# Scaling a broadcast matrix by fp32 row factors: eight small products or one, and which engine empties PSUM

## Chip, core and metric

The kernel runs on one core of one Trainium2 chip. The metric is the time of one execution on the device, in microseconds (us); the median of several executions is given. A core has TensorE (matrix products, results in PSUM), VectorE (DVE in the profile), ScalarE (ACT), GpSimd (POOL) and SyncE (SP); the last two mainly start DMA transfers in the part that matters here.

## The reference

Four layers act on x, which has 2048 rows of 1024 bf16 values. Layers A multiply a two-dimensional Fourier transform by a filter; layers B are a dense network with the Mish activation. Each works on the normalised rows.

```python
def _A_ref(x, w_r, w_i):
    X = rfft2(x.astype(float32))          # over rows and columns
    X = X * (w_r + 1j * w_i)
    return irfft2(X, s=(S, D)).astype(bfloat16)

def _B_ref(x, w1, b1, w2):
    h = x @ w1 + b1                        # 1024 -> 3584
    act = h * tanh(softplus(h))
    return act @ w2                        # 3584 -> 1024

x = x + _A_ref(layernorm(x), A_w_r, A_w_i)
x = x + _B_ref(layernorm(x), B_w1, B_b1, B_w2)
x = x + _A_ref(layernorm(x), A_w_r, A_w_i)
x = x + _B_ref(layernorm(x), B_w1, B_b1, B_w2)
```

## The kernel before

The Fourier transform is done as matrix products with constant tables. The first step, `s1`, takes 128 products of 128x128 matrices: for each n, `XR[:, n, :]` (a slice of x) with one constant matrix `M0`. In the first layer x comes straight from the input and is not yet normalised. Rather than normalise x, the kernel scales the matrix: `MN[:, n, :] = M0 * rc[:, n]`, where `rc` is fp32 and holds one factor for every partition and every n (1 over the standard deviation of a row). So 128 scaled copies of `M0` have to be made, in 16 blocks of eight.

`first_scales` computes the statistics of the rows and leaves the factors in `RT`:

```python
self.op(dve, lambda e: e.tensor_copy(rt.ap, self.RS[:, 2, :].unsqueeze(2).to_broadcast([P, 16, 8])), ...)   # L557
self.group([lambda e: e.transpose(self.PS[:, 7, 0:P], rt.ap..., self.IDF.ap)], ...)                          # L560
self.op(dve, lambda e: e.tensor_copy(rt.ap..., self.PS[:, 7, 0:P]), ...)                                     # L562
```

`scaled(j)` makes the eight matrices of block j, two thirds of them on VectorE and one third on ScalarE:

```python
def scaled(self, j):
    rt = self.RT
    rc = rt.ap.rearrange("p a b -> p (a b)")
    for q in range(8):
        n = 8 * j + q
        if q % 3 == 1:
            self.op(self.act, lambda e, n=n: e.activation(self.MN.ap[:, n, :], self.M0.ap, ACT.Copy, scale=rc[:, n:n + 1]), ...)        # L576
        else:
            self.op(self.dve, lambda e, n=n: e.tensor_scalar(self.MN.ap[:, n, :], self.M0.ap, rc[:, n:n + 1], None, op0=ALU.mult), ...) # L579
```

`s1` makes the matrices of four blocks ahead. For each block it runs eight products into a pair of PSUM banks (four pairs in rotation), moves the 1024 results of each partition to `Y` in SBUF as bf16, and makes the matrices of the block four further on. In the second layer A (`li` is 1) x is already normalised, and one matrix `M` serves for all.

```python
def s1(self, li):
    ...
    for j in range(4 if not li else 0):
        self.scaled(j)
    for j in range(16):
        ps, banks, _ = self.pair()
        for q in range(8):
            n = 8 * j + q
            m = M[:] if li else self.MN.ap[:, n, :]
            # matmul(ps[:, q * P:(q + 1) * P], XR.ap[:, n, :], m)                                   L594
        self.group(fns, reads=[self.r_xr[j // 4], self.r_m if li else self.r_mn[j]], writes=banks)
        ...
        if j % 2 or li and j == 8:
            # activation(dst, src, ACT.Copy): ScalarE empties the pair                               L600
        else:
            # tensor_copy(dst, src): VectorE empties the pair                                        L602
        if not li and j + 4 < 16:
            self.scaled(j + 4)
```

`[... cut ...]` After `s1` comes the transform along the other axis, `s2` (matmuls L675, evacuated by ScalarE at L710), which reads all of `Y`; the filter's rows, copied by VectorE (L899) and turned by TensorE (L888); the later steps (L720 to L798, among them the bf16 products with the filter on VectorE, L731 to L738); and a round trip through `u_scratch` in HBM. Its results go into x at L933, and the dense layer follows (L994 and L1012).

Of the kernel before, what the change touches and what calls it, by code (L numbers as in the profile page):

```python
# [6 lines left out]
ALU = mybir.AluOpType  # L7
P = 128
# [171 lines left out]
class KB:  # L180
# [389 lines left out]
    def scaled(self, j):  # L570
        rt = self.RT
        rc = rt.ap.rearrange("p a b -> p (a b)")
        for q in range(8):
            n = 8 * j + q
            if q % 3 == 1:
                self.op(self.act, lambda e, n=n: e.activation(self.MN.ap[:, n, :], self.M0.ap, ACT.Copy, scale=rc[:, n:n + 1]),  # L576
                        reads=[rt.res, self.M0.res], parts=[self.r_mn[j]])
            else:
                self.op(self.dve, lambda e, n=n: e.tensor_scalar(self.MN.ap[:, n, :], self.M0.ap, rc[:, n:n + 1], None, op0=ALU.mult),  # L579
                        reads=[rt.res, self.M0.res], parts=[self.r_mn[j]])  # L580

    def s1(self, li):
        self.Y = self.alloc("Y", self.o["Y"], [P, P])
        self.Y.res.begin()
        M, XR = self.M, self.XR
# [4 lines that stand above are left out]
            fns = []  # L590
# [3 lines that stand above are left out]
                fns.append(lambda e, q=q, n=n, ps=ps, m=m: e.matmul(ps[:, q * P:(q + 1) * P], XR.ap[:, n, :], m,  # L594
                                                                   start=True, stop=True))
            self.group(fns, reads=[self.r_xr[j // 4], self.r_m if li else self.r_mn[j]], writes=banks)
            src = ps.rearrange("p (q k) -> p k q", q=8)
            dst = self.Y.ap[:, :, 8 * j:8 * j + 8]
            if j % 2 or li and j == 8:
                self.op(self.act, lambda e, dst=dst, src=src: e.activation(dst, src, ACT.Copy), reads=banks, parts=[self.Y.res])  # L600
            else:
                self.op(self.dve, lambda e, dst=dst, src=src: e.tensor_copy(dst, src), reads=banks, parts=[self.Y.res])  # L602
            if not li and j + 4 < 16:
                self.scaled(j + 4)
        for r in ([self.MN.res, self.M0.res] + self.r_xr if not li else []):
            r.r(self.pe, self.pe.count)
            self.XR.res.r(self.pe, self.pe.count)
# [593 lines left out]
```

## Time and profile before

| | |
|---|---|
| time, median of 3 | 1047.37 us (1046.68 to 1048.07) |
| span of the profiled execution | 1044.8 us |
| TensorE busy | 951.7 us, 91% of the span |
| VectorE busy | 350.9 us, 34% |
| ScalarE busy | 336.4 us, 32% |
| mean granted TensorE clock | 0.971 of full speed |

The profile names each group of instructions by the line of the kernel, the engine, the operation, and output and input by buffer: most SBUF tiles lie in one large buffer and appear as ARENA, and PSUM as PS. Each row gives the count, the busy time, the mean duration of one, and how long the engine stood idle before them. Neighbouring instructions of one engine overlap a little, so their spacing is shorter than their duration. The chain is the path that ended last: at each step, what released the work, or what stood ahead of it on its engine. The granted clock is the share of full speed that TensorE was given. A view by windows gives the busy time of each engine in a stretch of the span.

### The profile page before, as it was taken

How to read it: one execution, taken by the hardware profiler on the slowest of the kernel's cores; microseconds unless marked ns; L12 is line 12 of the kernel's file. 1: busy time of each engine (PE TensorE's matmuls, PEld its weight loads, DVE VectorE, ACT ScalarE, POOL GpSimd, SP SyncE). 2: the span in 40 equal slices, each digit the busy share in tenths (PEclk: the TensorE clock that was granted, in tenths of full speed). 3: DMA queues.
4: the chain of work that ended last, by engine and by line, in shares of the span. 5: the costliest groups of instructions: out<-in, count | busy, mean ns of one | idle time of the engine just before them, and what ended most of it. 6: DMA issues, size and time to landing. Idle time of an engine off the chain costs nothing.

```text
span 1044.8 us, 14118 instructions
## 1 busy us (share of the span) xinstructions
PE 951.7 (91%) x5944; PEld 510.5 (49%) x6033; DVE 350.9 (34%) x776; ACT 336.4 (32%) x503; POOL 71.1 (7%) x114
## 2 busy tenths in 40 slices
PE   0799489999999999999979957999999999999998
PEld 0567465444444444444447736644444444444443
DVE  6888462431433100033337756426011100000111
ACT  6898163332000333400009834533300013440000
POOL 3242000000000000001621200000000000000000
PEclk9699789999999999999989988999999999999999
DMA  9779822464111121001941874145611112200000
GB/s 284 172 252 284 194 80 91 152 195 139 46 52 43 51 81 41 1 11 40 219 84 64 231 190 126 42 151 182 195 26 45 45 64 81 61 1 11 21 21 31
DMA packets 153055, 107.02 MB, mean 102 GB/s; under 512 B 74384, under 2 KB 132064, under 8 KB 152992
## 3 DMA queue, kind: packets, MB, share of 16 engines
q1 hardware_dynamic: 141472, 77.04, 26.0%
q0 software_dynamic: 9488, 27.68, 9.0%
q10 hardware_dynamic: 2032, 1.39, 0.5%
q8 instruction: 48, 0.79, 0.3%
q14 instruction: 15, 0.12, 0.0%
HBM read 80.85 MB, written 20.71 MB: 97 GB/s over the span
## 4 chain that ended last, share of the span: by engine, by line
PE 80%; DVE 9%; ACT 6%; DMA 3%; issue 1%; ACTq 0%; DVEq 0%
PE PS L994 37%; PE PS L1012 37%; DVE BN L460 2%; ACT ARENA L727 2%; PE PS L675 2%; DVE XS L933 1%; DVE ARENA L579 1%; DVE ARENA L796 1%; DMA ARENA<-u_scratch 1%; DMA u_scratch<-ARENA 1%; ACT ARENA L710 1%; DVE ARENA L969 1%; DVE ARENA L602 1%; PE PS L919 1%; ACT ARENA L798 1%
## 5 line engine op out<-in xcount | busy, mean ns | idle before, releaser
L994 PE MATMUL PS<-ARENA 128*128 128x512 bf16 (+1 forms) x1946 | 391.0, 360 | 10.3 <-DVE ARENA L969 7.2
L1012 PE MATMUL PS<-ARENA 128*128 128x512 bf16 x1756 | 385.5, 379 | 1.9
L998 ACT ACTIVATE ARENA<-PS,B 128x512 bf16<-128x512 f32 (+1 forms) x248 | 159.8, 646 | 438.8 <-PE PS L994 438.7
L994 PEld LDWEIGHTS PS<-ARENA 128*128 128x128 bf16 x1984 | 194.2, 99 | 202.2 <-DVE ARENA L969 8.7
L1012 PEld LDWEIGHTS PS<-ARENA 128*128 128x128 bf16 x1792 | 175.4, 98 | 211.4
L1017 DVE TENSOR_TENSOR XS<-PS,XS 128x512 bf16<-128x512 f32 x64 | 44.3, 692 | 537.9 <-PE PS L1012 537.9
L460 DVE BATCH_NORM_STATS2 BN<-XS 128x6 f32<-128x512 bf16 x104 | 67.2, 675 | 7.6 <-DMA XS<-in_A_x_dram 6.3
L933 DVE TENSOR_TENSOR XS<-PS,XS 128x512 bf16<-128x512 f32 (+1 forms) x40 | 29.1, 790 | 82.9 <-PE PS L919 82.9
L919 PE MATMUL PS<-MT,ARENA 128*128 128x32 bf16 (+1 forms) x768 | 24.3, 187 | 27.4 <-DMA ARENA<-u_scratch 24.7
L919 PEld LDWEIGHTS PS<-MT,ARENA 128*128 128x128 bf16 x768 | 22.9, 100 | 30.8 <-issue 25.0
L441 ACT ACTIVATE ARENA<-XS 128x1024 bf16<-128x1024 bf16 x24 | 25.3, 1055 | 37.3 <-DVE XS L933 32.4
L727 ACT ACTIVATE ARENA<-PS 128x1024 bf16<-128x1024 f32 x32 | 33.9, 1060 | 8.5 <-PE PS L723 8.5
L675 PE MATMUL PS<-FD,ARENA 128*128 128x256 bf16 (+1 forms) x256 | 33.8, 279 | 2.9 <-ACT ARENA L600 1.2
L756 ACT ACTIVATE ARENA<-PS 128x1024 bf16<-128x1024 f32 x32 | 33.9, 1061 | 3.7 <-PE PS L749 3.7
L432 ACT ACTIVATE RS<-MV,EPS 128x1 f32<-128x1 f32 (+1 forms) x7 | 2.0, 292 | 98.7 <-DVE MV L463 96.2
L749 PE MATMUL PS<-ARENA 128*128 128x256 bf16 x256 | 33.2, 273 | 0.1
L249 POOL DMA_DIRECT2D xn_scratch<-ARENA x12 | 6.5, 543 | 391.0 <-DVE ARENA L499 391.0
L731 DVE TENSOR_TENSOR ARENA<-ARENA 128x1024 bf16<-128x1024 bf16 x32 | 22.0, 687 | 22.0 <-ACT ARENA L727 22.0
L749 PEld LDWEIGHTS PS<-ARENA 128*128 128x128 bf16 x256 | 24.5, 98 | 10.0 <-DVE ARENA L738 1.2
L675 PEld LDWEIGHTS PS<-FD,ARENA 128*128 128x128 bf16 x256 | 24.6, 101 | 8.4 <-DVE ARENA L602 2.8
L770 PE MATMUL PS<-ARENA,BD 128*128 128x256 bf16 x192 | 25.9, 273 | 1.3 <-DVE ARENA L796 1.0
L499 DVE TENSOR_SCALAR ARENA<-XS,MV,RS 128x1024 bf16<-128x1024 bf16 x48 | 25.0, 543 | 1.0
(70 smaller groups left out, 502.8 us busy)
## 6 DMA issues: line engine op xcount, KB each, us to landing
ARENA<-in_B_w_dram SPq DMA_DIRECT2D x56, 512.0 KB, 4.0
ARENA<-in_B_w_dram SPq DMA_DIRECT2D x56, 256.0 KB, 4.5
u_scratch<-ARENA SPq DMA_DIRECT2D x14, 512.0 KB, 3.6
ARENA<-u_scratch SPq DMA_DIRECT2D x14, 512.0 KB, 5.7
XS<-in_A_x_dram SPq DMA_DIRECT2D x4, 1024.0 KB, 8.6
w_scratch<-ARENA POOLq DMA_DIRECT2D x8, 512.0 KB, 5.6
ARENA<-w_scratch POOLq DMA_DIRECT2D x8, 512.0 KB, 5.4
out_dram<-XS SPq DMA_DIRECT2D x16, 256.0 KB, 2.1
```

Of the source, the lines that this page charges most:

```text
L460: self.op(self.dve, lambda e: e.bn_stats(self.BN[:, j, 6 * h:6 * h + 6], self.XS[:, j, 512 * h:512 * h + 512]), reads=[self.r_xs[j]], part ...
L675: fns.append(lambda e: e.matmul(dst, at(r), FD[:, t:t + n], start=start, stop=stop))
L727: self.op(act, lambda e: e.activation(x.ap.rearrange("p a b -> p (a b)"), ps, ACT.Copy, scale=SIG), reads=banks, writes=[x.res])
L749: fns.append(lambda e, c=c, part=part: e.matmul(ps[:, c * 256:(c + 1) * 256], yk.ap[:, part, c * P:(c + 1) * P], t[:, (128, 0)[part]:(384, ...
L756: self.op(act, lambda e: e.activation(v.ap[:, :, i, :], src, ACT.Copy), reads=banks, parts=[v.res])
L770: fns.append(lambda e, dst=dst, part=part, c=c: e.matmul(dst, BD[:, c:c + P], mov(kd, part), start=(part == 0), stop=(part == 1)))
L919: fns.append(lambda e, l=l: e.matmul(ps[:, w * l:w * l + w], self.UT.ap[:, u0 + l, :], self.MT[:, 8 * lo:8 * lo + w], start=True, stop=True))
L933: self.op(self.dve, lambda e: e.tensor_tensor(xs, src, xs, ALU.add), reads=rb, parts=self.r_xs[lo:lo + nb])
L994: fns.append(lambda e, db=db, bank=bank, fl=fl: e.matmul(PS[:, bank, 0:w], wb.ap[:, db, fl * P:(fl + 1) * P], x.ap[:, db, tok], start=(db ...
L998: self.op(act, lambda e, bank=bank, ft=ft: e.activation(at.ap[:, ft, tok], PS[:, bank, 0:w], ACT.Mish, bias=self.B1[:, ft:ft + 1]), reads= ...
L1012: fns.append(lambda e, i=i, ft=ft: e.matmul(PS[:, bank, :], at.ap[:, ft, t * P:(t + 1) * P], W2[ft].ap[:, h * 512:(h + 1) * 512], start=(i ...
L1017: self.op(dve, lambda e: e.tensor_tensor(xs, PS[:, bank, :], xs, ALU.add), reads=[self.r_bank[bank]], writes=[self.r_xs[j]])
```

## The change

The eight matrices of a block are made by a single VectorE instruction: `M0` repeated eight times along a new middle axis, times the eight factors, each repeated along the inner axis. Blocks 3 and 11 are made by ScalarE alone, with eight instructions each. In the first layer, blocks 0 to 13 are evacuated by ScalarE, and 14 and 15 by VectorE; the second layer A is left as it was. The aim is to replace many short VectorE instructions by a few long ones, and to spread the work of `s1` over both engines in the new proportion.

```diff
     def scaled(self, j):
         rt = self.RT
         rc = rt.ap.rearrange("p a b -> p (a b)")
-        for q in range(8):
-            n = 8 * j + q
-            if q % 3 == 1:
+        if j % 8 == 3:
+            for n in range(8 * j, 8 * j + 8):
                 self.op(self.act, lambda e, n=n: e.activation(self.MN.ap[:, n, :], self.M0.ap, ACT.Copy, scale=rc[:, n:n + 1]),
                         reads=[rt.res, self.M0.res], parts=[self.r_mn[j]])
-            else:
-                self.op(self.dve, lambda e, n=n: e.tensor_scalar(self.MN.ap[:, n, :], self.M0.ap, rc[:, n:n + 1], None, op0=ALU.mult),
-                        reads=[rt.res, self.M0.res], parts=[self.r_mn[j]])
+        else:
+            n = slice(8 * j, 8 * j + 8)
+            self.op(self.dve, lambda e: e.tensor_tensor(self.MN.ap[:, n, :], self.M0.ap.unsqueeze(1).to_broadcast([P, 8, P]),
+                                                        rc[:, n].unsqueeze(2).to_broadcast([P, 8, P]), ALU.mult),
+                    reads=[rt.res, self.M0.res], parts=[self.r_mn[j]])
@@ in s1
-            if j % 2 or li and j == 8:
+            if (j % 2 or j == 8) if li else j < 14:
                 self.op(self.act, lambda e, dst=dst, src=src: e.activation(dst, src, ACT.Copy), reads=banks, parts=[self.Y.res])
             else:
                 self.op(self.dve, lambda e, dst=dst, src=src: e.tensor_copy(dst, src), reads=banks, parts=[self.Y.res])
```

The change adds one line, so below `scaled` each line number of the changed kernel is one higher: L602 becomes L603, L675 becomes L676, and so on. The new product stands on L579.

## The prediction

> **What bounds the kernel now.** I read the page's table of 40 slices first: from the fourth slice on TensorE is busy nearly throughout, and the two dense products of the B layers are 74% of the chain that ended last. The changed lines touch none of that. They lie in the first 47 us, so the question is what ends last between about 24 and 47 us. The chain, cut to that stretch, answers it:
>
> ```profile
> 24.19 3.34 DVE ARENA L579 x20
> 27.53 1.13 DVE ARENA L602
> 28.66 1.62 DVE ARENA L579 x10
> 30.29 1.13 DVE ARENA L602
> ...
> 42.45 1.63 DVE ARENA L579 x10
> 44.07 2.27 DVE ARENA L602 x2
> 46.34 0.05 issue
> 46.39 1.89 PE PS L675 x8
> ```
>
> Columns are start, length, and what held the chain. From 24.19 to 46.34 us it never leaves VectorE: 80 small scalings (L579, in packs of 20 and six of 10) and 8 evacuations (L602). Spacing inside the packs is 1.63 / 10 = 0.163 us a scaling; an evacuation takes 1.13 us. So 80 x 0.163 + 8 x 1.13 = 22.1 us, which is the whole stretch. The groups of 24 to 46.4 us, shapes kept apart, show the other engines (columns: count, busy us and mean ns, idle us before and its releaser):
>
> ```profile
> L576 ACT ACTIVATE ARENA<-ARENA 128x128 bf16<-128x128 bf16 x48 | 14.8, 394 | 1.5 <-DVE ARENA L562 1.5
> L594 PE MATMUL PS<-ARENA 128*128 128x128 bf16 x128 | 14.1, 292 | 7.4 <-DVE ARENA L579 5.5 <-ACT ARENA L600 1.1 <-ACT ARENA L576 0.8
> L579 DVE TENSOR_SCALAR ARENA<-ARENA 128x128 bf16<-128x128 bf16 x80 | 13.6, 251 | 0.0
> L602 DVE CAST ARENA<-PS 128x1024 bf16<-128x1024 f32 x8 | 9.6, 1211 | 0.0
> L600 ACT ACTIVATE ARENA<-PS 128x1024 bf16<-128x1024 f32 x8 | 8.1, 1014 | 0.6 <-PE PS L594 0.6
> ```
>
> VectorE's rows have 0.0 idle. ScalarE is nearly as full (14.8 + 8.1 us). TensorE waits mostly for L579. One more view matters, the busy time by windows (length; PE, weight loads, DVE, ACT, POOL busy; granted clock; DMA share; GB/s):
>
> ```profile
> 24.00:33.00 9.00, 5.51 (x56) 4.48 (x56) 8.96 (x44) 8.81 (x26) 0.00 (x0) 1.00 1.15 265
> 33.00:42.00 9.00, 6.23 (x54) 5.31 (x55) 9.00 (x35) 9.00 (x26) 5.31 (x9) 0.50 0.95 210
> 42.00:46.00 4.00, 2.33 (x21) 1.76 (x18) 4.00 (x13) 3.42 (x6) 0.00 (x0) 0.50 0.35 139
> 46.00:50.00 4.00, 3.61 (x19) 2.59 (x20) 2.90 (x5) 1.95 (x4) 0.28 (x1) 0.50 0.02 4
> ```
>
> The granted clock is 0.50 from about 33 until 50 us (half-microsecond windows put its return between 50.0 and 50.5). DMA has almost nothing left to do after 44 us.
>
> [...] L731, a 1024-element bf16 product with one broadcast operand, averages 686 ns and its successors follow 0.61 us later. No row of this trace has a 1024-element product with an fp32 operand in SBUF. The nearest is L933, fp32 from PSUM plus bf16: four in 4.63 us, 1.16 us each. [...] 128 elements cost 0.163 us in L579, whereas 1024 cost 1.13 us in L602, so eight small scalings (1.30 us) cost more than one slow pass over as much data. [...] L576 agrees: 394 ns each, 15 in 4.49 us, i.e. one every 0.30 us. [...] The trace shows the 0.50 stretch[...].
>
> **The change, part by part.** *Scaling.* VectorE loses 80 scalings of 0.163 us = 13.0 us. It gains 14 products of 1024 elements. [...] the spacing of L602 and L933, 1.13 to 1.16 us, so 1.14 us each (an estimate from those two rows), 16.0 us in all. The inner step of zero should not hurt: L557, a broadcast fp32 copy of 128 elements, took 0.23 us. ScalarE's scalings fall from 48 to 16 (blocks 3 and 11): 16 x 0.30 = 4.8 us.
>
> *Evacuation.* VectorE keeps two of eight: 2 x 1.13 = 2.3 us. ScalarE has 14 in place of 8. Its back-to-back spacing in the chain after 50 us is 0.92 us: 14 x 0.92 = 12.9 us. VectorE then has 16.0 + 2.3 = 18.3 us of work and ScalarE 4.8 + 12.9 = 17.7 us, against 22.1 and about 22 now.
>
> *Do they interlock?* I walked the instruction order of the changed kernel forward from 24.19 us. VectorE issues its 14 products without a wait between them, and both evacuations come last. So block 0's matrices are ready at 25.3, block 1's at 26.5, block 2's at 27.6, block 10's at 35.6, block 15's at 40.15. ScalarE scales block 3 first (to 26.6), then evacuates blocks 0 to 7 at 0.92 us each (26.6 to 34.0), scales block 11 (to 36.4), and evacuates 8 to 13 (to 41.9). A block's eight matmuls take 0.65 us at full clock and 0.95 us at half (16 in 1.89 us at 35 to 45 us). Block 1 is transformed by 27.2 and wanted at 27.5; block 2 by 28.3 and wanted at 28.4: tight, but without a stall. There are four pairs of PSUM banks, so block 14 needs the pair of block 10, free at 39.1, and block 15 that of block 11, free at 40.0. Block 14 is transformed at about 40.1 and VectorE, finished at 40.15, evacuates it to 41.3. Block 15 is done at 41.2, evacuated to 42.45. The stage ends at about 42.5 where it now ends at 46.34: **3.8 us saved**.
>
> *After the stage.* The next transform begins at once (L675), and its first half runs at half clock. Now that lasts from 46.39 to about 50.1, 3.7 us. [...] The filter rows that VectorE copies next were requested at 34.7 to 37.6 us and took up to 5.8 us to land, i.e. until about 42.7 for the second pair, which is wanted at 43.8: no wait. Behind that ScalarE, VectorE and then the DMA round trip at 112 to 124 us follow one another, and nothing there is tied to absolute time, so the gain passes on. Layer A's second pass keeps its rule for who evacuates. 3.8 - 0.25 gives 3.55.
>
> **Rivals.** (1) *The fp32 broadcast product is slower[...].* [...] 14 x 2.2 = 31 us, the stage would end near 57 us, 11 us later than now: 1058. For it: no such row exists. Against: L933 and L557. If on the contrary it ran [...] (0.61 us), nothing more is gained, because ScalarE's chain to 41.9 and the banks it frees set the end.
>
> (2) *ScalarE becomes the bound, or the two fall out of step.* The totals, 17.7 and 18.3, lie so close that any stall of ScalarE counts. Block 11's scalings stand ahead of six evacuations, and each late one delays the bank for 14 and 15. Were its evacuation 1.0 us, as its duration reads, the end would move by about 1.1 us: 1045.
>
> (3) *The gain is lost downstream.* If the clock still returns only at 50.1 us, 7.6 us run at half speed in place of 3.7. If TensorE were then the sole bound, half of the extra 3.9 us would go: saved 1.9, so 1045.5. For it: half the stage after s1 now waits for TensorE at 0.50. [...]
>
> **Range and chances.** 1047.37 - 3.55 = 1043.8. Rivals 2 and 3 reach 1045 to 1046; less than 1042 would need a stage of 16 us, below both engines' totals, and only run-to-run spread (1.4 us here) could show that. So 1042.2 to 1045.8. A change of 2% is 21 us, which is the length of the whole stage; faster by that 0.01, within 2% 0.98, slower 0.01[...].
>
> **What would show it right or wrong.** Right: 14 VectorE products of mean 1.1 to 1.25 us, the last ending near 40.2; the chain in this stretch passing between VectorE and ScalarE; first L676 matmul at about 42.6 us; the stretch from there to the u_scratch round trip as long as now. Wrong: products of 2 us or more; ScalarE idle before its evacuations by over 1 us in sum; the first matmul of the next stage after 44; or the 0.50 clock lasting to 50 us, with the distance from that matmul to the round trip grown by more than 0.5 us.

## The result, and the profile after

The changed kernel took 1042.66 us (1041.26 to 1043.27), the kernel before 1047.71 us in the same comparison. The ratio is 0.9951, with a 95% interval of 0.9934 to 0.9969: 5.1 us less (3.2 to 6.9). The prediction was 1043.8 us.

The groups of 24 to 42.5 us, shapes kept apart, answer to those shown of before (count; busy us and mean ns; idle us before and its releaser):

```profile
L579 DVE TENSOR_TENSOR ARENA<-ARENA 128x1024 bf16<-128x1024 bf16 x14 | 16.0, 1216 | 0.0
L601 ACT ACTIVATE ARENA<-PS 128x1024 bf16<-128x1024 f32 x14 | 13.3, 1049 | 0.2
L595 PE MATMUL PS<-ARENA 128*128 128x128 bf16 x128 | 11.2, 246 | 6.1 <-DVE ARENA L579 3.5 <-ACT ARENA L601 2.0 <-ACT ARENA L575 0.5
...
L575 ACT ACTIVATE ARENA<-ARENA 128x128 bf16<-128x128 bf16 x16 | 4.9, 410 | 1.5 <-DVE ARENA L562 1.5
L603 DVE CAST ARENA<-PS 128x1024 bf16<-128x1024 f32 x2 | 2.4, 1218 | 0.1
```

Neither VectorE nor ScalarE has an idle gap worth naming, and both have about four microseconds less to do. Their order in time, from the timeline (start, length, what; pieces of one kind merged):

```profile
24.05 15.98 DVE L579 TENSOR_TENSOR ARENA<-ARENA 128x1024 bf16<-128x1024 bf16 x14
...
26.47 7.81 ACT L601 ACTIVATE ARENA<-PS 128x1024 bf16<-128x1024 f32 x8
...
34.11 2.46 ACT L575 ACTIVATE ARENA<-ARENA 128x128 bf16<-128x128 bf16 x8
...
36.45 5.61 ACT L601 ACTIVATE ARENA<-PS 128x1024 bf16<-128x1024 f32 x6
...
40.11 2.35 DVE L603 CAST ARENA<-PS 128x1024 bf16<-128x1024 f32 x2
...
42.52 1.05 PE L676 MATMUL PS<-FD,ARENA 128*128 128x256 bf16 x8 [1.53 <-DVE ARENA L603]
```

The next transform starts at 42.52 us, where it started at 46.39: 3.87 us earlier. Its eight matmuls take 1.05 us, where they took 1.89. That is full clock in place of half, and the windows agree:

```profile
33.00:42.00 9.00, 4.89 (x64) 3.65 (x64) 8.92 (x9) 9.00 (x16) 5.09 (x8) 1.00 0.88 182
42.00:46.00 4.00, 3.48 (x32) 2.86 (x32) 3.05 (x5) 2.46 (x5) 0.07 (x1) 1.00 0.60 226
46.00:50.00 4.00, 3.64 (x25) 2.27 (x24) 0.99 (x2) 4.00 (x7) 3.68 (x7) 1.00 0.52 118
```

A useful second mark is the first matmul behind the round trip through HBM (L919 before, L920 after): 123.86 us before, 119.04 after, so 4.82 us earlier. Of these, 3.87 were won before the next transform and 0.95 between it and the round trip. The two profiled spans differ by only 3.3 us. Behind the mark the instructions are the same in both kernels, so the other 1.5 us are put down to chance; that is not shown.

The clock's share can be read close to its cause. The fifth group of eight matmuls of the next transform starts 7.69 us behind the first before, and 6.45 us in the changed kernel, 1.24 us less:

```profile
54.08 1.04 PE L675 MATMUL PS<-FD,ARENA 128*128 128x256 bf16 x8
48.97 1.04 PE L676 MATMUL PS<-FD,ARENA 128*128 128x256 bf16 x8
```

Behind that the changed kernel loses some of it. GpSimd waits for the transfer of B1 (the bias b1 of the dense layer, which it converts), and the request for the third pair of filter rows stands behind that wait in its queue, so TensorE waits for these rows:

```profile
POOL B L415 <- DMA B1h<-in_B_b_dram: 5.9, 1, 5.9
PE PS L889 <- DMA ARENA<-in_A_w_i_dram: 1.0, 1, 1.0
```

For each experiment below, this table has the start of the next transform (the end of the stage), the time of its first eight matmuls, the time from the first group of eight to the fifth, the mark behind the round trip, and the distance from the start to the mark, all read from the timelines. From the first group to the fifth, six kernels take 6.44 to 6.46 us; the others met half clock there and take 7.31 us or more (e11 also waits for filter rows). In e8 and e11 the clock fell only behind the first eight: the next sixteen took 2.98 and 3.06 us, against 1.69 in the changed kernel.

| kernel | next transform, us | its 8 matmuls, us | first to fifth group, us | mark, us | distance, us |
|---|---|---|---|---|---|
| before | 46.39 | 1.89 | 7.69 | 123.86 | 77.5 |
| changed | 42.52 | 1.05 | 6.45 | 119.04 | 76.5 |
| e1 changed again | 42.65 | 1.05 | 6.46 | 119.02 | 76.4 |
| e2 scaling alone | 49.35 | 1.89 | 7.74 | 126.82 | 77.5 |
| e3 evacuation alone | 51.90 | 1.89 | 8.42 | 130.03 | 78.1 |
| e4 conversion moved | 42.60 | 1.89 | 7.38 | 119.91 | 77.3 |
| e5 before again | 46.49 | 1.89 | 8.20 | 124.45 | 78.0 |
| e6 before, products twice | 46.47 | 1.03 | 6.44 | 122.74 | 76.3 |
| e7 changed, products twice | 44.49 | 1.05 | 6.46 | 120.76 | 76.3 |
| e8 four blocks on GpSimd | 46.34 | 1.04 | 7.55 | 123.61 | 77.3 |
| e9 bf16 factors | 42.90 | 1.89 | 7.31 | 119.86 | 77.0 |
| e10 bf16 factors in pairs | 42.45 | 1.05 | 6.46 | 119.48 | 77.0 |
| e11 pairs, work shared | 38.28 | 1.05 | 10.60 | 119.88 | 81.6 |
| e12 and constants late | 38.04 | 1.05 | 6.45 | 115.85 | 77.8 |

### The profile page after: what moved, and what is told of

Read it like the earlier page. It is cut to its first block, busy times and chain, and to the rows that moved or that the text cites. A ratio compares the mean times of both kernels' runs of the same rounds, so it can differ in the third digit from the quotient of the medians.

```text
span 1041.5 us, 14145 instructions
## 1 busy us (share of the span) xinstructions
PE 953.4 (92%) x6033; PEld 508.4 (49%) x6033; DVE 347.2 (33%) x704; ACT 333.1 (32%) x477; POOL 70.9 (7%) x114
## 4 chain that ended last, share of the span: by engine, by line
PE 82%; DVE 6%; ACT 4%; DMA 3%; SPq 3%; issue 2%; POOL 1%; ACTq 0%; DVEq 0%; POOLq 0%
PE PS L995 37%; PE PS L1013 37%; SPq L249 3%; PE PS L676 1%; DVE XS L934 1%; ACT ARENA L728 1%; DVE ARENA L797 1%; DMA ARENA<-u_scratch 1%; DMA u_scratch<-ARENA 1%; DVE ARENA L970 1%; PE PS L920 1%; PE PS L771 1%; PE PS L750 1%; ACT ARENA L799 1%; ACT ARENA L601 1%
## 5 line engine op out<-in xcount | busy, mean ns | idle before, releaser
L995 PE MATMUL PS<-ARENA 128*128 128x512 bf16 (+1 forms) x1984 | 395.1, 361 | 8.3 <-DVE ARENA L970 7.2
L920 PE MATMUL PS<-MT,ARENA 128*128 128x32 bf16 (+1 forms) x768 | 24.4, 187 | 27.3 <-DMA ARENA<-u_scratch 24.7
L920 PEld LDWEIGHTS PS<-MT,ARENA 128*128 128x128 bf16 x768 | 23.1, 100 | 30.8 <-issue 24.9
L676 PE MATMUL PS<-FD,ARENA 128*128 128x256 bf16 (+1 forms) x256 | 32.4, 271 | 2.8 <-DVE ARENA L603 1.5
L676 PEld LDWEIGHTS PS<-FD,ARENA 128*128 128x128 bf16 x256 | 23.9, 98 | 7.5 <-DVE ARENA L603 3.1
```

The source lines that it names most:

```text
L676: fns.append(lambda e: e.matmul(dst, at(r), FD[:, t:t + n], start=start, stop=stop))
L920: fns.append(lambda e, l=l: e.matmul(ps[:, w * l:w * l + w], self.UT.ap[:, u0 + l, :], self.MT[:, 8 * lo:8 * lo + w], start=True, stop=True))
L995: fns.append(lambda e, db=db, bank=bank, fl=fl: e.matmul(PS[:, bank, 0:w], wb.ap[:, db, fl * P:(fl + 1) * P], x.ap[:, db, tok], start=(db ...
```

## The experiments

The theory: the stage lasts as long as the fuller of two engines, and the change pays because it lowers the sum of their work and divides it evenly. Rivals: the broadcast product is the gain by itself; relieving VectorE of evacuations is; or the gain beyond the stage belongs to the clock and to chance.

### Each part alone (e2, e3)

e2 takes the new `scaled` and leaves the evacuation rule as it was; e3 the reverse.

```diff
 e2, in s1 of the changed kernel
-            if (j % 2 or j == 8) if li else j < 14:
+            if j % 2 or li and j == 8:
 e3, in s1 of the kernel before
-            if j % 2 or li and j == 8:
+            if (j % 2 or j == 8) if li else j < 14:
```

> Broadcast products as in the changed kernel, evacuation shared by odd and even blocks as before. Theory (the stage lasts as long as the fuller engine): VectorE then has 14 x 1.14 + 8 x 1.13 = 25.0 us and ScalarE 4.9 + 7.4 = 12.3, so the stage ends near 24.05 + 25.0 = 49.1 us, 2.7 us later than in the kernel before: about 1050 us, slower. Rival (the broadcast product is itself the gain, the evacuation rule an addition): faster than before by 2 us or more.

> Eight small scalings per block as before, evacuation of blocks 0 to 13 by ScalarE. Theory (fuller engine): ScalarE has 48 x 0.30 + 14 x 0.93 = 27.4 us, VectorE 80 x 0.163 + 2 x 1.13 = 15.3; the stage ends near 51.5 us, 5 us later than before: about 1052 us, slower. Rival (VectorE's evacuations were the hindrance, and relieving it pays by itself): faster than before by 2 us or more.

Measured: e2 1050.06 us, ratio to before 1.0026 (1.0015 to 1.0036); e3 1052.65 us, ratio 1.0050 (1.0038 to 1.0063). Each half of the change makes the kernel slower. The groups of e2 up to 49 us:

```profile
L579 DVE TENSOR_TENSOR ARENA<-ARENA 128x1024 bf16<-128x1024 bf16 x14 | 16.5, 1218 | 0.0
...
L603 DVE CAST ARENA<-PS 128x1024 bf16<-128x1024 f32 x8 | 9.7, 1217 | 0.0
L601 ACT ACTIVATE ARENA<-PS 128x1024 bf16<-128x1024 f32 x8 | 8.2, 1024 | 12.0 <-PE PS L595 11.9
```

and of e3 up to 51.5 us:

```profile
L600 ACT ACTIVATE ARENA<-PS 128x1024 bf16<-128x1024 f32 x14 | 14.2, 1022 | 0.0
...
L602 DVE CAST ARENA<-PS 128x1024 bf16<-128x1024 f32 x2 | 2.4, 1224 | 11.9 <-PE PS L594 11.9
```

In e2 ScalarE stands idle for 12.0 us while VectorE never does; in e3 it is VectorE that waits, for 11.9 us. The stage ended at 49.35 and 51.90 us, where the sums of the fuller engine gave 49.1 and 51.5. Both rivals that saw the gain in one part alone fall.

### The same kernels again (e1, e5)

Nothing is edited.

> The changed kernel once more, for a second profile of it. Theory A (the clock stays up because the products of the first transform now come evenly[...]): the granted clock is again 1.00 from 33 to 46 us, and the next transform again starts near 42.5 us. Rival B[...]: this time the clock shows 0.50 somewhere between 30 and 50 us. The wait for the third pair of filter rows (1.0 us before L889 in the first profile) is expected again if it is caused by the order of the POOL queue; it is gone if it was a matter of when the small B1 transfer happened to land.

> The kernel before once more, for a second profile. If the 0.50 clock from 33 to 50 us comes from how TensorE is used in this stretch[...], it comes again[...]. If it is chance, it is absent or much shorter this time.

e1 took 1041.53 us, e5 1047.66 (one execution each). In e1 the stage and the clock were as in the first profile. TensorE's wait for the third pair of filter rows was gone: the B1 transfer had landed at 39.4 us (45.9 in the first profile). So that wait does not come in every execution, and by the table (76.5 against 76.4) most of its 1.0 us at TensorE was made up before the mark. It may cost more: in e10, where B1 landed at 46.4 us, the path that ended last leads through this wait, and the distance is 77.0 us at full clock. In e5 the half clock came again, but the clock column does not show it. The window and the matmuls of e5:

```profile
46.00:50.00 4.00, 3.51 (x18) 2.51 (x19) 3.00 (x5) 1.95 (x4) 0.18 (x1) 1.00 0.02 4
```

```profile
46.49 1.89 PE L675 MATMUL PS<-FD,ARENA 128*128 128x256 bf16 x8 [1.19 <-DVE ARENA L602]
```

A clock of 1.00 is recorded, yet eight matmuls of 256 columns take 1.89 us as they did at 0.50. From here on the clock is judged by durations of matmuls.

### GpSimd's conversion out of the way (e4)

```diff
 in constants(), removed, and placed behind the loop over steps in layer_A
-        self.op(self.pool, lambda e: e.tensor_copy(self.B1[:], self.B1h[:]), reads=[r], writes=[self.r_b1])
```

> The changed kernel, with the small GpSimd conversion of B1 (L415, which waits for a transfer of 2-byte pieces) moved behind all filter and table loads of the layer. Theory (that conversion holds up the GpSimd queue, so the third pair of filter rows is requested 2.4 us late and TensorE waits 1.0 us for it): rows requested near 44.1 us, no wait before L889, total 1.0 us less than the changed kernel, about 1041.7 us. Rival (the rows are late anyway, by the DMA engines, or ScalarE's chain hides the wait): no change against 1042.7 us.

Measured: 1042.9 us (1040.83 to 1045.23), ratio 0.9951 (0.9937 to 0.9965). The expected gain of 1.0 us is not seen, though with this spread it hardly could be, and the profiled execution differs from the first profile in its clock as well: with the same stage up to 42.6 us, the next transform ran at half clock.

```profile
42.60 1.89 PE L676 MATMUL PS<-FD,ARENA 128*128 128x256 bf16 x8 [1.54 <-DVE ARENA L603]
```

So the evenness of the changed kernel does not protect the clock in every execution; theory A of e1 is too strong.

### More work for TensorE (e6, e7)

```diff
-                fns.append(lambda e, ...: e.matmul(ps[:, q * P:(q + 1) * P], XR.ap[:, n, :], m, start=True, stop=True))
+                for _ in range(1 if li else 2):
+                    fns.append(lambda e, ...: e.matmul(ps[:, q * P:(q + 1) * P], XR.ap[:, n, :], m, start=True, stop=True))
```

> The kernel before, with each of the 128 products of the first transform done twice in a row into the same place (same result, twice the work for TensorE, which is idle there for 40% of the time). Theory ([...] half the clock costs the next transform up to 1.8 us): the stage still ends near 46.3 us, set by VectorE; the clock stays at 1.00 until then; the next transform's first half takes about 1.5 to 1.8 us less, and the total falls to about 1045.6 us. Rival (the half clock hides behind ScalarE's evacuations and costs nothing): the clock stays up, and the total stays within 0.4 us of before. Second rival (the drop has another cause): the clock drops all the same, and the doubled products, about 1.8 us a block at half clock, are still hidden.

> The changed kernel with each product of the first transform done twice. Theory: the clock stays up in every run, where it dropped in one of three profiles so far; the stage ends near 42.5 us as before (a block takes 1.1 us, just under VectorE's 1.14 and ScalarE's 0.93 plus waits: up to 0.5 us later is possible); total 1042 us, with less spread than the 2.0 us of the changed kernel. Rival (the changed kernel's evenness alone keeps the clock up, so nothing is left to gain): no change, or slower by the time the doubled products add, 0.5 to 1.5 us.

e6: 1046.8 us, ratio 0.9991 (0.9985 to 0.9998). A kernel with 128 useless matmuls more is 0.9 us faster (0.2 to 1.6). The stage ended where it did, and the next transform ran at full clock:

```profile
46.47 1.03 PE L676 MATMUL PS<-FD,ARENA 128*128 128x256 bf16 x8 [1.16 <-DVE ARENA L603]
```

Its distance to the mark was 76.3 us against 77.5 and 78.0 in the two profiles of before, and from the first group to the fifth it took 6.44 us against 7.69 and 8.20, so all of this is still there at the mark. With more work for TensorE the next transform thus ran at full clock (1.03 us for its first eight matmuls against 1.89), and the half clock costs the next stage 1.2 to 1.8 us. The profile is of one execution, but that of e7 shows full clock as well, and the lower total of e6, from 22 executions, goes the same way. The total fell by about half of what was expected; whether some executions of before keep the full clock, or part of the gain is lost behind the mark, is not known.

e7 missed: 1045.1 us, ratio to before 0.9978 (0.9970 to 0.9986), 2.4 us more than the changed kernel, and the stage ended at 44.49 us, not at 42.5 to 43. ScalarE's first evacuations show why:

```profile
27.26 1.02 ACT L602 ACTIVATE ARENA<-PS 128x1024 bf16<-128x1024 f32 x1 [0.83 <-PE PS L596]
28.97 1.02 ACT L602 ACTIVATE ARENA<-PS 128x1024 bf16<-128x1024 f32 x1 [0.68 <-PE PS L596]
30.20 1.94 ACT L602 ACTIVATE ARENA<-PS 128x1024 bf16<-128x1024 f32 x2 [0.21 <-PE PS L596]
```

The first doubled block took from 25.36 to 27.26 us, 119 ns a matmul. That is the rate of half clock (118 ns in the kernel before at a recorded 0.50, 16 in 1.89 us), though the record shows 1.00 here; later in e7 80 took 4.80 us, 60 ns each. ScalarE waited 0.83 + 0.68 + 0.21 = 1.7 us, and began block 11's matrices at 35.64 us, 1.5 us later than in the changed kernel. With two engines this evenly full, a stall early in ScalarE's row is handed on to the end.

### A third engine (e8)

```diff
+    GP = (5, 8, 11, 14)          # issued in first_scales, ahead of the filter loads
-            self.op(self.dve, lambda e: e.tensor_tensor(...))
+            self.op(self.pool if j in self.GP else self.dve, lambda e: e.tensor_tensor(...))
 block 3 alone on ScalarE; VectorE's products ahead of the loop; VectorE evacuates 11 and 13
```

> The changed kernel with blocks 5, 8, 11 and 14 scaled by GpSimd, which is idle there, one broadcast product each; block 3 by ScalarE; all of VectorE's products issued ahead of its evacuations, which are blocks 11 and 13. Theory A (GpSimd is a third engine beside the two): VectorE has 11 x 1.14 + 2 x 1.13 = 14.8 us, ScalarE 2.4 + 14 x 0.93 = 15.4, and the stage ends near 39.7 us, 2.7 us earlier than in the changed kernel: about 1040 us. Theory B[...]: the times add on VectorE. [...]

Measured: 1046.89 us, ratio 0.9993 (0.9985 to 1.0002), no better than before. The groups up to 46 us:

```profile
L583 DVE TENSOR_TENSOR ARENA<-ARENA 128x1024 bf16<-128x1024 bf16 x11 | 19.4, 1832 | 0.0
L606 ACT ACTIVATE ARENA<-PS 128x1024 bf16<-128x1024 f32 x14 | 13.6, 1027 | 6.3 <-PE PS L600 6.1
...
L583 POOL TENSOR_TENSOR ARENA<-ARENA 128x1024 bf16<-128x1024 bf16 x4 | 11.4, 2884 | 2.0 <-DVE ARENA L562 2.0
```

VectorE's 11 products took 19.4 us where 11 x 1.14 = 12.5 would do. From 24.0 to 35.4 us both engines worked and finished four blocks each, 2.85 us a pair; VectorE alone makes a block in 1.14 us. The longest VectorE product took 2.92 us, the shortest 1.21. So theory A falls, and the stage ended at 46.34 us. Why the two engines slow each other is not shown. VectorE lost 6.9 us while GpSimd worked for 11.4; what a GpSimd product takes by itself was not measured, so whether the times add in full, as theory B has it, can't be told.

### What sets the product's rate, and what a faster one brings (e9, e10)

```diff
 e9: factors copied to bf16
-                                                        rc[:, n].unsqueeze(2).to_broadcast([P, 8, P]), ALU.mult)
+                                                        self.RB.ap[:, n].unsqueeze(2).to_broadcast([P, 8, P]), ALU.mult)
 e10: each bf16 factor stored twice, RB is [P, 128, 2]; M0 and MN viewed in pairs as well
+    self.M0.ap.rearrange("p (a b) -> p a b", b=2).unsqueeze(1).to_broadcast([P, 8, 64, 2]),
+    self.RB.ap[:, n, :].unsqueeze(2).to_broadcast([P, 8, 64, 2]), ALU.mult)
```

> The changed kernel with the factors rounded to bf16 (another small copy of 128 elements ahead; the factors lose precision), each still repeated along the inner axis. Theory A, as the prediction had it[...]: now all operands are bf16, and a product takes 0.61 us, as L731 does; VectorE has its 14 products done near 33 us instead of 40. Theory B ([...] here the factor's inner step is zero): still 1.14 us each. The stage ends near 42.5 us in either case, 0.2 us later for the extra copy, since ScalarE's chain and the banks it frees set the end.

> As the run before, but every bf16 factor is stored twice side by side, so that the inner axis of all operands is two neighbouring elements. Under theory B this alone brings 0.61 us a product; under theory A it changes nothing against the run before. If it is 0.61 us, VectorE is done with its products near 33 us and waits for PSUM, ScalarE's order is unchanged, and the end of the stage stays near 42.5 us (+0.3 for the copy of 256 elements): about 1043 us. That the end does not move although the broadcast product takes half the time is what the prediction claimed of this case; the rival is that the stage shortens with VectorE's work, by 3 us or more, to 1039 us.

e9 took 1042.31 us (one execution); e10 1043.01 us, ratio 0.9959 (0.9944 to 0.9975). Their products, first e9 and then e10:

```profile
L582 DVE TENSOR_TENSOR ARENA<-ARENA 128x1024 bf16<-128x1024 bf16 x14 | 16.0, 1217 | 0.0
```

```profile
L583 DVE TENSOR_TENSOR ARENA<-ARENA 128x1024 bf16<-128x1024 bf16 x14 | 8.5, 682 | 0.0
L608 DVE CAST ARENA<-PS 128x1024 bf16<-128x1024 f32 x2 | 2.4, 1220 | 7.1 <-PE PS L600 7.1
```

With bf16 factors the product is as slow as with fp32 (1217 and 1216 ns); with bf16 factors and an inner step of one it takes 682 ns. Fp32 factors with an inner step of one were not tried. VectorE gained 7.5 us in e10 and spent 7.1 of them waiting for PSUM: the stage ended at 42.45 us, as before.

### A version that shares the freed time (e11, e12)

e11 has the pairs of e10, scales only block 3 on ScalarE, issues all products ahead of the loop and lets VectorE evacuate blocks 8, 10, 12 and 14. Both kernels round the factors to bf16.

```diff
 e11
-            if (j % 2 or j == 8) if li else j < 14:
+            if (j % 2 or j == 8) if li else j not in (8, 10, 12, 14):
 e12, besides: M, BD, MT, IDENT and B1 are requested behind the first filter, as in
-        self.dma(sp, self.BD[:], self.con["BD"], "bd", writes=[self.r_bd])
+        self.dma(sp, self.BD[:], self.con["BD"], "bd", reads=after, writes=[self.r_bd])      # after = [WT[0].res]
```

> As the run before with the freed VectorE put to use: only block 3 is scaled by ScalarE, all products are issued ahead, and VectorE evacuates blocks 8, 10, 12 and 14. At 0.61 us a product VectorE has 0.3 + 15 x 0.61 + 4 x 1.13 = 14.0 us and ScalarE 2.4 + 12 x 0.92 = 13.4 us: end of the stage near 38.5 us (TensorE at half clock could make it 39.5), 4 us before the changed kernel: about 1039 us. If a product takes 1.14 us, VectorE has 21.9 us and the stage ends near 46.5: about 1047 us.

> The previous kernel (bf16 factors in pairs, both engines sharing the work) ended its first transform at 38.3 us, 4.2 us before the changed kernel, and yet took as long: TensorE and VectorE then waited until 42.2 us for the first pair of filter rows. Here the tables that nothing needs until 60 us or later (M, BD, MT, IDENT, 0.5 MB, and B1 in 2-byte pieces) are requested only once the first filter is made, and the conversion of B1 on GpSimd stands behind the other loads. Theory (these transfers share the DMA engines with the filter rows at 34 to 42 us, where the engines are busy all the time at under 270 GB/s): the rows land near 39 us, the wait falls from 3.9 us to under 1, and the total is 3 us less than the changed kernel, about 1039.5 us. Rival (the rows are bound by their own request, at 34.9 us behind the last slice of x, and their own pieces): they land after 41 us again, and the total stays at about 1042.5 us.

e11: 1042.95 us, ratio 0.9958 (0.9945 to 0.9970). The stage ended at 38.28 us, close to the 38.5 expected, and nothing came of it. The timeline of e11:

```profile
38.28 1.05 PE L679 MATMUL PS<-FD,ARENA 128*128 128x256 bf16 x8 [1.20 <-DVE ARENA L608]
39.37 1.02 ACT L714 ACTIVATE ARENA<-PS 128x1024 bf16<-128x1024 f32 x1 [1.22 <-PE PS L679]
42.16 1.37 DVE L903 COPY ARENA<-ARENA 128x1024 bf16<-128x1024 bf16 x2 [3.93 <-DMA ARENA<-in_A_w_i_dram]
```

The first filter rows arrive at 42.16 us. TensorE, idle for 2.85 us until then, also ran its next sixteen matmuls largely at half clock (3.06 us against 1.69). The changed kernel, ending its stage at 42.5, stands just behind this wait without showing it. e12 took the constants out of the rows' way, and they arrived at 39.3 us. It took 1041.32 us (1038.88 to 1043.29), ratio 0.9942 (0.9929 to 0.9956). Its mark is 3.2 us earlier than in the changed kernel, and the execution that it was read from took 1039.09 us. But the median is only 1.3 us lower, and the intervals of the two ratios overlap. It beats the kernel before; that it beats the changed one is likely and not shown. The expected 1039.5 us was missed. Why, stays open, apart from TensorE's waits of 2.3 and 0.2 us for rows that now follow too slowly.

## Why the prediction was right

**The stage.** Predicted end "about 42.5 us", measured 42.52. The forward walk holds piece by piece: VectorE's products were to be done at 40.15 (40.03), ScalarE's evacuations to run from 26.6 (26.47), block 11 to be scaled from 34.0 (34.11), the last six evacuations to begin at 36.4 (36.45). 3.8 us were predicted and 3.87 measured (3.73 if each kernel is counted from its own first scaling, at 24.19 and 24.05 us). The "two thirds" and "one third" of the section on the kernel before are 80 and 48 of the 128 scalings, five and three of each eight. e2 and e3 show that it is the balance that pays, as rival 2 implied, and e7 that a stall of ScalarE is not absorbed.

**The product's cost.** 1.14 us a piece was right (15.98 / 14). That the factors are fp32 is not the whole of it: e9 has the same rate with bf16 factors (1217 ns), and e10, with bf16 factors too but an inner step of one in place of zero, has 682 ns. The sentence "The inner step of zero should not hurt" is therefore wrong for bf16; beside fp32 it was not tested.

**A faster product: "nothing more is gained".** e10 ran at 682 ns and ended its stage at 42.45 us.

**After the stage.** This is the term that failed. The 0.25 us that the prediction takes off the 3.8 was the author's estimate for a longer stretch at half clock. In the profiled execution the clock did not fall (1.05 us for the first eight matmuls), and the stretch to the round trip, expected as long as before, was 0.95 us shorter. In four profiles with this stage (changed, e1, e4, e9) the next transform ran at full clock twice and at half clock twice, in both of before at half. Even where it was half, in e4 and e9, it was back by 46.0 us (1.00 in the window from 46 to 50 us, and four matmuls of 256 columns in 0.61 and 0.62 us at 46.93 and 47.15, against 1.06 at half clock), some 3 us behind the start; their distances, 77.3 and 77.0 us, are no longer than before. So none of the four shows the charge. What decides between full and half in the same stage stays open; in e6 and e7, with more work for TensorE, it was full (1.03 and 1.05 us). The sum 3.87 + 0.95 = 4.8 us lies within the measured 3.2 to 6.9, but so does 3.55. How often the clock falls in each kernel was not counted, so the share of it in the 5.1 us is an estimate. That the total came within 1.1 us rests on the stage.

**Downstream.** "No wait" for the second pair of filter rows held in that profile. The margin was thinner than the text made it seem: e11 puts the first pair at 42.16 us, 0.4 us before the stage ended. The sentence "nothing there is tied to absolute time" did not hold: the third pair, which it leaves out, came 1.0 us late behind B1.

## What to carry to other kernels

When two engines share a stage, add up the work of each and walk their order forward; a change that moves work between them must be judged whole, for its halves may each make things worse. A stage can be shortened only down to the next thing that arrives, here filter rows at 42 us: look for the transfer that lands just before the stage ends. And the idle time of TensorE is worth a look even where it is not the bottleneck: here it stood idle for 7.4 of 22 us in the kernel before, whose next eight matmuls took 1.89 us; with the products doubled they took 1.03.

## What the runs showed of the hardware

- The recorded clock can be silent on a halved clock: 1.00 in e5 where eight matmuls of 256 columns took 1.89 us, against 1.05 at full clock.
- In one and the same stage the clock fell in some executions and not in others: of four profiles, two show eight matmuls of the next transform in 1.05 us and two in 1.89 us.
- A product of 1024 elements with an innermost step of zero took 1217 ns in bf16, and 682 ns with the same factors stored twice and read in pairs.
- GpSimd and VectorE products together gave one block each in 2.85 us, slower than VectorE alone, which makes two in 2.28 us.
- Doubling 128 matmuls in a stage that waits for other engines made the kernel 0.9 us faster (0.2 to 1.6).
